# Attention with a deeper lag between scores and transposed probabilities: (1, 5, 7) to (1, 6, 8), eight probability tiles, a fourth conversion buffer

## The chip, the cores and the metric

The kernel runs on one core of one Trainium2 chip. The metric is the device time of one execution in microseconds. Three executions of the kernel before took 909.98, 910.92 and 910.42 us (median 910.42). Times and the trace are of one core; its engines are TensorE (PE, with its weight loads PEld), VectorE (DVE), ScalarE (ACT), GpSimd (POOL), and SyncE (SP), which issues most transfers.

## What is computed

Three layers follow one another: block-causal attention, a feed-forward layer with a squared ReLU, and a layer of eight experts of which each token takes one.

```python
# q, k, v: (4, 8, 576, 64); x: 2304 tokens x 512
scores = scale * np.matmul(q, k.transpose(0, 1, 3, 2))
scores = np.where(block_i >= block_j, scores, -1e9)       # blocks of 64 positions
attn = np.exp(scores - np.max(scores, axis=-1, keepdims=True))
attn = attn / (np.sum(attn, axis=-1, keepdims=True) + 1e-09)
x = (attn @ v)  # heads side by side -> (2304, 512)
g = s * np.maximum(x @ w_in, 0.0) ** 2 + b                # w_in 512 x 2048, float64 on arrival
x = g @ w_out
# then: gate, argmax over 8 experts, out[mask] = gate * (relu(x[mask] @ w1[e]) @ w2[e])
```

## The kernel before

**Attention.** Two heads of one batch make a unit `u`; there are 16 units. A unit has nine query blocks `i` of 64 rows (two heads side by side fill 128 rows), so there are 144 pairs `(u, i)`, and block `i` has `64 * (i + 1)` keys. The loop at L230 takes one step `t` for each pair, and a few steps more to empty the pipeline. In a step it calls, in this order:

- `p_transpose` for the pair `LT` steps back (L231 to L235): PE transposes the probabilities by chunks of 128 keys (L185) into one of three PSUM banks, and ACT copies them to SBUF (L191). Blocks 0 to 3 go in twos.
- `scores` for the pair of this step (L238): POOL zeroes the ragged end of the probability tile (L135), PE multiplies (L143 or L146, three passes) into one of four PSUM banks, DVE takes the maximum (L148, for the last block two halves and L151), ACT takes the exponential with its sum (L153). The last block takes two banks.
- in steps 4 to 6 of a unit the transposes of the next unit's q and k (L93, L123), and the loads of later units on SP (L75, L76, for v with a POOL memset at L67).
- `normalise` for the pair `LN` steps back (L255): DVE forms the reciprocal of the sum (L162 or L164, then L165), POOL multiplies the tile by it (L166).
- `pv` for blocks 3 and 8 of the unit `LP` steps back (L258 to L261): PE multiplies the transposed probabilities by v (L208), ACT copies the result (L210), and after block 8 SP stores the unit (L213).

The lags are in one line, with the number of probability tiles below it:

```python
LAGS = (1, 5, 7)     # LN, LT, LP (L279)
NPBUF = 6            # buffers of the pool a_p, tag "p" (L280)
```

**The feed-forward layer beside it.** The kernel's main loop (L310) runs one step of attention and then, at steps 8, 12, ..., 80 (`CONV`), one step of `convert` (L361): a weight chunk arrives as float64 (L327 on SP), three integer instructions on DVE make float32 of it (L336 to L338, into a tile of the pool `cv`), ACT rounds it to a high part (L371), and POOL subtracts to get the low part (L342). The three stages of one chunk stand in three successive conversion steps. From step 50 on, one "piece" is put behind an attention step every 2.8 steps: a load of 256 tokens (L318, L321, L322), a hidden group (`hidden`, 24 matmuls at L385, then L395 to L398), or a projection (L460). There are 40 pieces; the last ones follow the attention loop. Then `after` (L488) runs the rest of the layer, starting with tokens of the last batch, which need every unit stored.

**Order.** The framework places instructions on the engines' queues when the program is built, earlier program order first among what it reckons ready; on the chip each queue is in order. SBUF tiles of one pool and tag share that pool's buffers, and a new tile waits until its buffer's last reader is done.

Of the kernel before, what the change touches and what calls it, by code (L numbers as in the profile page):

```python
# [20 lines left out]
def attention(nc, tc, ctx, ps, ident, q, k, v, xT_d):  # L21
# [15 lines left out]
    kt = pool("a_kt", 2)  # L37
    pp = pool("a_p", NPBUF)
    small = pool("a_small", 8)
# [175 lines left out]

    LN, LT, LP = LAGS
    QK, V = (("q", q), ("k", k)), (("v", v),)
# [58 lines left out]
            setattr(self, n, ctx.enter_context(p))  # L276


LAGS = (1, 5, 7)  # L279
NPBUF = 6  # L280
PTBUF = 1
BANKS_0 = (4, 3, 1)
P_COPY = lambda nc, i: nc.scalar.copy
# [2 lines left out]
class SquaredRelu:  # L286
# [175 lines left out]

    def beside(self, ctx, blocks):

        self.pools(ctx, "a", 1, 2, max(NA), "raw cv xr x r g")
        rows = ctx.enter_context(self.tc.tile_pool(name="ma_rows", bufs=1))
        return self._beside(blocks, rows)

# [108 lines left out]
NA = (2, 4, 4, 4, 4, 4)  # L577
# [802 lines left out]
```

## Time and profile before

| | us |
|---|---|
| median of three executions | 910.42 |
| the profiled execution | 910.26 |
| its span, first to last instruction | 908.6 |
| time around the span | 1.7 |
| PE busy in the span | 878.3 (97%) |
| DVE busy | 640.3 (70%) |
| ACT busy | 569.9 (63%) |
| POOL busy | 219.9 (24%) |

Attention runs from the start to about 328 us. The granted TensorE clock is at full speed throughout (0.998 of it in the mean). Busy time in the table is a union over the instructions of an engine; an engine's idle time stands before the instruction that it waited with, and the engine and line whose end released it follow the arrow.

### The profile page before, as it was taken

The numbers are of one execution on the slowest core, as the hardware profiler recorded it, in microseconds if no ns is written. First come the engines' busy times: TensorE is split into PE (matmuls) and PEld (weight loads), VectorE is DVE, ScalarE is ACT, GpSimd is POOL, SyncE is SP. The second block draws the span as 40 slices with busy tenths as digits, with TensorE's granted clock in tenths as the row PEclk, the third lists the DMA queues.
The fourth block names the chain that finished last, engine by engine and source line by source line (L and its number), as shares of the span: only waits on it lengthen the run. The fifth ranks groups of instructions, "written<-read, shape, count | busy, mean of one in ns | idle before, by whom it ended". The sixth has DMA issues, their size and how long they took to land. (4 is left out here: it accounts for less than half of the span.)

```text
span 908.6 us, 17050 instructions
## 1 busy us (share of the span) xinstructions
PE 878.3 (97%) x5765; PEld 725.4 (80%) x5765; DVE 640.3 (70%) x1490; ACT 569.9 (63%) x1165; POOL 219.9 (24%) x335
## 2 busy tenths in 40 slices
PE   6889999999999999999999999999999999999996
PEld 5666777888878789999999999998467776776775
DVE  5889986464645446878967777767688887776782
ACT  6888786575757544333566655542288777776773
POOL 4677675142333200000000000002025322222110
PEclk9999999999999999999999999999999999999999
DMA  5766543322221133445212212115346796637500
GB/s 138 181 178 184 143 116 78 100 53 76 77 72 29 53 109 104 157 140 175 59 47 69 71 61 60 47 47 190 119 139 232 239 386 236 224 129 257 188 24 28
DMA packets 109481, 113.84 MB, mean 125 GB/s; under 512 B 62679, under 2 KB 80617, under 8 KB 109387
## 3 DMA queue, kind: packets, MB, share of 16 engines
q1 hardware_dynamic: 105579, 100.74, 35.3%
q0 software_dynamic: 3808, 11.94, 3.7%
q8 instruction: 48, 0.79, 0.4%
q14 instruction: 46, 0.38, 0.1%
HBM read 143.58 MB, written 19.80 MB: 180 GB/s over the span
## 5 line engine op out<-in xcount | busy, mean ns | idle before, releaser
L385 PE MATMUL ph<-xh,wih 128*128 128x256 f32 x576 | 165.9, 288 | 0.0
L385 PE MATMUL ph<-xh,wil 128*128 128x256 f32 x576 | 162.2, 282 | 0.0
L385 PE MATMUL ph<-xl,wih 128*128 128x256 f32 x576 | 162.0, 281 | 0.0
L166 POOL TENSOR_TENSOR p<-p,rc 128x64 f32<-128x64 f32 (+2 forms) x144 | 111.5, 783 | 119.8 <-DVE rc L165 56.7
L385 PEld LDWEIGHTS ph<-xh,wih 128*128 128x128 f32 x576 | 109.0, 189 | 5.3 <-issue 3.1
L385 PEld LDWEIGHTS ph<-xl,wih 128*128 128x128 f32 x576 | 109.2, 189 | 1.1
L385 PEld LDWEIGHTS ph<-xh,wil 128*128 128x128 f32 x576 | 109.2, 190 | 0.4 <-issue 0.4
L148 DVE TENSOR_REDUCE nm<-sc 128x1 f32<-128x288 f32 (+8 forms) x160 | 70.4, 450 | 54.3 <-PE sc L146 46.1
L153 ACT ACTIVATE p<-sc,nm 128x288 f32<-128x288 f32 (+8 forms) x160 | 80.6, 507 | 18.5 <-DVE nm L148 8.0
L1009 DVE TENSOR_TENSOR w1l<-raw,w1h 128x1024 fp32r<-128x1024 f32 x60 | 71.7, 1223 | 22.8 <-ACT w1h L1008 17.8
L1009 DVE TENSOR_TENSOR w2l<-raw,w2h 128x1024 fp32r<-128x1024 f32 x64 | 75.2, 1220 | 9.6 <-ACT w2h L1008 9.5
L1017 POOL DMA_INDIRECT xr<-x_d,gidx_e x2 | 2.3, 1130 | 310.4 <-PE ph L385 310.1
L185 PE MATMUL tp<-ident,p 128*128 128x128 f32 x400 | 65.3, 278 | 6.8 <-POOL p L166 4.9
L395 ACT ACTIVATE r<-ph 128x512 f32<-128x512 f32 x44 | 26.3, 597 | 72.0 <-PE ph L385 71.9
L1008 ACT CAST w2h<-raw 128x1024 fp32r<-128x1024 f32 x64 | 66.1, 1050 | 6.1 <-PE py L1106 5.9
L1008 ACT CAST w1h<-raw 128x1024 fp32r<-128x1024 f32 x60 | 61.6, 1051 | 9.4 <-PE ph L1091 8.7
L191 ACT COPY pt<-tp 128x512 f32<-128x512 f32 (+3 forms) x128 | 61.7, 499 | 8.8 <-PE tp L185 8.4
L185 PEld LDWEIGHTS tp<-ident,p 128*128 128x128 f32 x400 | 46.1, 142 | 18.7 <-POOL p L166 9.2
L396 DVE SCALAR_TENSOR_TENSOR r<-r,sc 128x512 f32<-128x512 f32 x44 | 34.7, 789 | 36.3 <-ACT r L395 36.0
L208 PE MATMUL o<-pt,raw_v 128*64 128x320 f32 (+4 forms) x448 | 55.9, 366 | 1.1 <-ACT pt L191 1.1
L1106 PE MATMUL py<-w2h,hh 128*128 128x512 f32 x128 | 51.6, 403 | 0.0
L1117 POOL DMA_INDIRECT out_dram<-y,sidx x15 | 19.8, 1323 | 130.5 <-ACT y L1073 128.7
(306 smaller groups left out, 2300.6 us busy)
## 6 DMA issues: line engine op xcount, KB each, us to landing
raw<-in_moe_w_dram SPq DMA_DIRECT2D x172, 512.0 KB
xr<-xT_d SPq DMA_DIRECT2D x19, 512.0 KB
wr<-in_moe_w_in_dram SPq DMA_DIRECT2D x16, 512.0 KB
wr<-in_moe_w_out_dram SPq DMA_DIRECT2D x16, 512.0 KB
row<-part_d SPq DMA_DIRECT2D x20, 256.0 KB
x_d<-row SPq DMA_DIRECT2D x18, 256.5 KB
xT_d<-x SPq DMA_DIRECT2D x16, 288.0 KB
raw_q<-in_q_dram SPq DMA_DIRECT2D x32, 128.0 KB
```

Source lines behind the costliest of these rows:

```text
L148: ps.last["max"] = nc.vector.tensor_reduce(nm[:, e:e + 1], sc[:, 0:w], AX.X, ALU.max, negate=True)
L153: ps.last["exp"] = nc.scalar.activation(pr[:, k0:k0 + w], scs[e][:, 0:w], AF.Exp, bias=nm[:, 0:1], accum_out=sm[:, e:e + 1])
L166: ps.last["scale"] = nc.gpsimd.tensor_mul(pr[:, 0:n], pr[:, 0:n], rc.to_broadcast([P, n]))
L185: nc.tensor.transpose(t[:, e * P:(e + 1) * P], st[u][i][0][:, c * P:(c + 1) * P], ident)
L191: P_COPY(nc, i0)(o, src)
L208: nc.tensor.matmul(o[r, first * D:n], vt[:, c, hh], p[:, first:, c, r], start=(c == 0), stop=(c == cs[-1]))
L385: nc.tensor.matmul(ph[:, e], self.wi[p][w][:, c, e * P:(e + 1) * P], x[a][:, c], start=(n == 0), stop=(n == 3 * KC - 1))
L395: nc.scalar.activation(r, ph.rearrange("p e (t n) -> p (e t) n", n=P), AF.Relu)
L396: nc.vector.scalar_tensor_tensor(r, r, self.sc[:, 0:1], r, ALU.mult, ALU.mult)
L1008: self.nc.scalar.copy(ws[0][c], r)
L1009: self.nc.vector.tensor_sub(ws[1][c], r, ws[0][c].bitcast(F32))
L1106: nc.tensor.matmul(py, hT[a][:, c], self.w2s[w][c // 2][:, c % 2 * D:c % 2 * D + D], start=(t == 0), stop=(t == 3 * KF - 1))
```

## The change

The lags become 1, 6 and 8: transposes are called six steps behind their scores and the product with v eight steps behind, two steps apart as before. The pool of probability tiles has eight buffers instead of six (each 2.5 KB in a partition). The pool `cv` of the conversion that runs beside attention has four buffers instead of three (each 2 KB). The conversion of the later stage keeps its two. The loop has one step more.

```diff
-LAGS = (1, 5, 7)
-NPBUF = 6
+LAGS = (1, 6, 8)
+NPBUF = 8
 PTBUF = 1
 BANKS_0 = (4, 3, 1)
...
     def beside(self, ctx, blocks):
 
-        self.pools(ctx, "a", 1, 2, max(NA), "raw cv xr x r g")
+        self.pools(ctx, "a", 1, 2, max(NA), "raw cv xr x r g", 4)
```

## Rows read from the trace of the kernel before

**Rows 1.** Busy us by stretch: stretch, length, PE, PEld, DVE, ACT, POOL, clock, DMA.
```profile
30.00:90.00 60.00, 51.45 (x372) 39.28 (x372) 53.14 (x167) 52.37 (x166) 42.97 (x72) 1.00 0.64 177
90.00:150.00 60.00, 57.31 (x412) 46.69 (x412) 50.79 (x159) 48.31 (x150) 41.82 (x70) 1.00 0.49 132
150.00:330.00 180.00, 179.76 (x1247) 150.61 (x1246) 90.00 (x273) 110.70 (x311) 52.32 (x101) 1.00 0.21 61
```

**Rows 2.** Groups of PE, 30 to 90 us: count, busy, mean ns, idle before, releasers.
```profile
L185 PE MATMUL tp<-ident,p 128*128 128x128 f32 x104 | 17.4, 280 | 5.5 <-POOL p L166 4.4 <-ACT pt L191 0.7 <-POOL wil L342 0.3
L208 PE MATMUL o<-pt,raw_v 128*64 128x320 f32 (+4 forms) x112 | 13.3, 366 | 1.1 <-ACT pt L191 1.1
L146 PE MATMUL sc<-kh,qh 128*128 128x288 f32 (+5 forms) x35 | 13.2, 376 | 1.2 <-ACT p L153 1.2
```

**Rows 3.** The same view of PE, 10 to 30 us.
```profile
L185 PE MATMUL tp<-ident,p 128*128 128x128 f32 x27 | 4.7, 283 | 0.5 <-POOL p L166 0.5
```

**Rows 4.** The same view of ACT and DVE, 30 to 90 us.
```profile
L153 ACT ACTIVATE p<-sc,nm 128x288 f32<-128x288 f32 (+8 forms) x40 | 20.1, 506 | 3.3 <-DVE nm L148 1.1 <-DVE rc L164 1.1 <-DVE rc L165 0.9
L191 ACT COPY pt<-tp 128x512 f32<-128x512 f32 (+3 forms) x32 | 15.2, 500 | 3.4 <-PE tp L185 3.3
...
L148 DVE TENSOR_REDUCE nm<-sc 128x1 f32<-128x288 f32 (+8 forms) x41 | 18.0, 452 | 4.0 <-PE sc L146 3.4 <-PE sc L143 0.4
L336 DVE TENSOR_SCALAR f<-wr 128x512 int32<-128x512 int32 x9 | 6.8, 759 | 1.1 <-POOL wol L342 1.1
```

**Rows 5.** Timeline: start, us, engine, line, [idle before]: first score, first hidden matmul.
```profile
7.71 0.95 PE L143 MATMUL sc<-kf,qf 128*128 128x64 f32 x3
...
89.67 0.36 PE L385 MATMUL ph<-xh,wih 128*128 128x256 f32 x1
```

**Rows 6.** Timeline round two of the waits for POOL, with the exponentials that free banks.
```profile
37.02 0.19 ACT L153 ACTIVATION_READ_ACCUMULATOR p<-sc,nm 128x1 f32 x1
37.79 0.33 PE L146 MATMUL sc<-kh,ql 128*128 128x384 f32 x1
38.96 0.77 PE L185 MATMUL tp<-ident,p 128*128 128x128 f32 x5 [0.83 <-POOL p L166]
...
51.75 0.33 PE L146 MATMUL sc<-kh,ql 128*128 128x384 f32 x1
52.73 0.19 ACT L153 ACTIVATION_READ_ACCUMULATOR p<-sc,nm 128x1 f32 x1
53.35 0.77 PE L185 MATMUL tp<-ident,p 128*128 128x128 f32 x5 [1.27 <-POOL p L166]
```

**Rows 7.** Timeline round a wait for an exponential.
```profile
33.90 0.68 DVE L338 SCALAR_TENSOR_TENSOR f<-wr,f 128x512 int32<-128x512 int32 x1
34.50 0.15 DVE L151 TENSOR_TENSOR nm<-nm 128x1 f32<-128x1 f32 x1
35.58 0.39 PE L146 MATMUL sc<-kh,qh 128*128 128x256 f32 x1 [1.17 <-ACT p L153]
```

**Rows 8.** One line's durations (ns min/median/max), 30 to 90 and 328 to 430 us.
```profile
L336 DVE TENSOR_SCALAR f<-wr x9: 401/696/1269, 32.0 to 81.2; 128x512 int32<-128x512 int32 x9
L336 DVE TENSOR_SCALAR f<-wr x16: 418/421/426, 328.4 to 425.5; 128x512 int32<-128x512 int32 x16
```

**Rows 9.** Timeline: a load of v, and the product of that unit.
```profile
59.72 0.20 POOL L67 MEMSET raw_v<- 64x128 f32 x1
...
76.83 0.87 PE L208 MATMUL o<-pt,raw_v 128*64 128x256 f32 x8
```

**Rows 10.** Timeline at the end of attention.
```profile
325.47 2.27 PE L208 MATMUL o<-pt,raw_v 128*64 128x320 f32 x20
...
330.67 0.37 SPq L318 DMA_DIRECT2D xr<-xT_d  x1
...
338.44 0.38 PE L385 MATMUL ph<-xh,wih 128*128 128x256 f32 x1
...
346.13 0.39 PE L460 MATMUL pxa<-woh,gl 128*128 128x512 f32 x1
```

## The prediction

> **What bounds the kernel now.** I read the busy times by stretch first [rows 1]. From 150 to 330 us PE is idle for 180 - 179.76 = 0.24 us: there PE's own work sets the pace, and the change takes none away and adds none. From 90 to 150 us PE is idle for 2.7 us, from 30 to 90 for 8.55 us. So whatever the change can win lies ahead of 150 us, and nearly all of it ahead of 90. A microsecond of PE idle time removed there is a microsecond of the kernel, since PE is full behind it.
>
> In the 60 us from 30 to 90 no engine is the plain bound: DVE is busy for 53.1 us, ACT for 52.4, PE for 51.45 [rows 1]. The next view is who makes PE wait there. Of the 8.55 us, 5.5 stand before the transposes of the probabilities, 4.4 of them for POOL's normalised tile and 0.3 for POOL's conversion; 1.1 stand before the product with v, 1.2 before scores that wait for an exponential to free a bank [rows 2]. In the 20 us before, 0.5 more are waits for POOL [rows 3]. The same standstill is seen from the other side on ACT and DVE: the copy of the transposes waits 3.3 us for PE, the maximum 3.8 us for scores that are queued behind the waiting transpose [rows 4]. So the loop is coupled: PE, held up by POOL, starves DVE and ACT, which in turn make POOL late.
>
> **The change part by part.** *The transposes one step later.* The first score starts at 7.71 us and the first hidden matmul, a piece of step 53, at 89.67 [rows 5], so a step takes (89.67 - 7.71)/53 = 1.55 us. The longest wait for POOL on PE's queue is 1.27 us [rows 6]; one step more of lag is longer than any of them, so this wait goes altogether: 4.4 + 0.3 + 0.5 = 5.2 us.
>
> What is late next? In place of the transposes PE would go on with the next scores, and those need a bank, of which there are four. Both stalls shown stand behind the scores of block 5; the next score, of block 6, takes the bank of block 2, which its exponential frees. In the first stall PE stands from 38.12 us (37.79 + 0.33) and that exponential is done at 37.21: the bank is free, and all of the 0.83 us is won. In the second PE stands from 52.08 and the exponential is done at 52.92, so only 53.35 - 52.92 = 0.43 of 1.27 us is won [rows 6]. Together 1.26 of 2.10, or 60%. I apply that to all: 0.6 x 5.2 = 3.1 us. A cap comes from the other engines: if ACT and DVE keep the rest of their idle time, the stage shrinks by the smaller of what they wait for PE, 3.3 and 3.8 us [rows 4]; 3.1 is just under it. The bounds are 0 (each wait replaced by one for a bank) and 5.2 us.
>
> *The product with v one step later, and the drain.* PE's work of one step, transposes and products, moves out of the stretch where PE has gaps into the one where it has none. By their busy times it is at most (17.4 + 13.3) us over 60/1.55 = 39 steps, 0.8 us [rows 2]. Against that, ACT's copies of one step move out of the same stretch, and ACT is short of time there. The bounds are 0 and +0.8; I take +0.6.
>
> At the end of attention, the last product ends at 327.7 us; its store, the load of the next tokens (issued at 330.67) and their rounding follow, and the first matmul on them comes at 338.44. PE fills this with pieces, which last until 346.5 [rows 10]. From 338.44 on there are still about 7 us of them. One step later in the program, the product changes places with at most one hidden piece, 24 matmuls, or 2.7 us at the 0.11 us apiece of that product (20 in 2.27 us). About 4 us of cover stay, so this costs nothing; with the cover gone it would be the rest of the 10.7 us chain. On SP the store is issued one step later, and what is queued behind it (a weight chunk and the token load) moves with it.
>
> *The v buffers.* A load of v may start when the product two units before is done, which now comes one step later; POOL's memset waits there with the normalising multiplies of the next blocks behind it, and on SP the loads behind v's wait too. The v loaded at 59.72 us is used at 76.83 [rows 9]; with 17 us between them a step of 1.55 us is hidden. The multiplies behind the memset have the extra step of lag themselves. 0, at worst +0.5 us.
>
> *Eight tiles instead of six.* A tile is now free again two or one steps before its next use, instead of one or none. It removes waits of POOL's memset and costs only memory. 0.
>
> *The fourth conversion buffer.* DVE waited once, 1.1 us, for POOL to be done with a conversion tile [rows 4]. That wait goes. PE had scores and transposes queued at the time, so between 0 and 1.1 us is won; I take 0.2, since DVE then only gets to its next wait sooner.
>
> The profiled execution took 910.26 us (span 908.6 and 1.7 around it), 0.16 us below the median. The sum: 910.26 - 3.1 + 0.6 - 0.2 = **907.6 us**.
>
> One row speaks for a smaller gain. The first conversion instruction takes 0.42 us in the stretch in which POOL is idle, and 0.76 in the mean, up to 1.27, from 30 to 90 us [rows 4, 8], where POOL is busy for 43 of 60 us [rows 1]: DVE loses 9 x 0.34 = 3 us on this line to POOL's presence. The Trainium skill has a rule for it (SBUF — State Buffer, "The single rule" and the notes on reading its diagram): VectorE and GpSimd share one pair of ports, held for a whole instruction, and the other engine blocks. By it a shorter stage packs the same POOL work more densely (5% more in 57 us), and of DVE's 3 us some 0.2 us more would be lost: 907.8 us. The trace's spread of 0.40 to 1.27 us for one shape agrees with it.
>
> **The rivals.** *The wait only changes its name (chance 0.27).* The planner's order moves, but PE then waits for exponentials, as in the second stall [rows 6], where two thirds of the time would be lost again; DVE and ACT, at 89 and 87%, are the loop's real pace. For it: both have 3 to 4 us of idle time that PE does not cause. Against it: the first stall, where the bank was free. Counting every stall as the second one (0.43 of 1.27) gives 1.8 us, less 0.6: 909.1 us; with none won, 910.9. Here belongs also that the planner already places transposes where it reckons them ready, so that one step more in the program moves little in the queues.
>
> *DVE's conversions hold up the exponentials (0.24, slower).* The three conversion instructions stand ahead of the combined maximum of a unit's last block; it ends at 34.65, the exponential waits for it, and PE stands for 1.17 us [rows 7]. With a conversion tile always free, the planner can place such a run earlier on DVE's queue, and with the lag changed it falls on other blocks. It happens in one unit of the four between 30 and 90 us. The price is 1.2 us for each unit hit; nine units are converted beside, up to 144 us. It decides from the third unit on, which eats the 2.7 us won. With five units hit: 907.6 + 4 x 1.2 = 912.4 us.
>
> *The loop comes loose (0.13).* All 5.2 us and the 1.1 us on DVE go, nothing takes their place: 904.0 us. Against it: DVE would be busy for 53.1 of 54 us, with ACT beside it at 97%.
>
> **How the numbers follow.** The forecast has 0.36, with a range of its own of 906.3 to 908.9. With 0.13 for the loose loop, 0.27 for the renamed wait (908.9 to 911) and 0.24 for the conversions (911 to 914), the range that holds 8 in 10 is 904.8 to 912.8: it leaves out some of the loose loop and the worse half of the conversions' case. A difference of 0.2%, 1.8 us, is about what a measurement of this kernel can tell from no change. Below 908.6 lie the loose loop and nearly all of the forecast: 0.47. Above 912.2 lie two thirds of the conversions' case and a little of the others, for orders that the trace of before cannot show: 0.19. Between them 0.34.
>
> **What would show it.** In the changed profile, between 30 and 90 us, the transposes' wait for POOL should be gone (4.4 to under 1 us), the scores' wait for the exponential should rise from 1.2 to about 3, ACT's wait for the transposes fall below 1.5 of its 3.3 us, and the first hidden matmul should come at about 87 instead of 89.7. DVE's wait for POOL's conversion should be gone. PE's idle time from 150 to 330 us should stay under 0.5 us, and the chain behind the last product should still be covered. Wrong would be: PE idle in 30 to 90 us as before with another name (first rival), or several waits for the exponential of a last block, one a unit (second). A change of PE's idle time behind 330 us would be something that I have not counted.

## The result: 916.2 us, 0.7% slower, all of it lost beside attention

The changed kernel took 916.17 us (median; 915.82 to 916.89), the kernel before 910.67 (six runs, 909.95 to 911.23): a ratio of 1.0069, 95% interval 1.0058 to 1.0080. I had forecast 907.6 us, with 904.8 to 912.8 as the range. The profiled execution took 916.09 us with a span of 914.4, 5.8 us more than before. (One execution of the changed kernel and one of `after_q_copies_late`, both at a throttled clock, are left out of ranges and ratios; the medians count them, which moves them by less than 0.3 us.)

First, where the time lies. Timelines of PE, the changed kernel: start in us, duration, engine, line.

```profile
89.91 0.28 PE L385 MATMUL ph<-xh,wih 128*128 128x256 f32 x1
...
331.06 2.27 PE L208 MATMUL o<-pt,raw_v 128*64 128x320 f32 x20
...
352.15 0.39 PE L460 MATMUL pxa<-woh,gl 128*128 128x512 f32 x1
```

The first hidden piece comes when it came before [rows 5]; the last product is 5.6 us later, the last projection beside attention 6.0 us later [rows 10]. The span is 5.8 us longer, so nothing is lost behind that: of the loss, 0.2 us stand ahead of the first hidden piece and some 5.4 between it and the last product. Busy time by stretch, in the columns of [rows 1]:

```profile
30.00:90.00 60.00, 53.78 (x372) 40.38 (x369) 55.21 (x168) 52.41 (x168) 44.29 (x68) 1.00 0.63 169
90.00:150.00 60.00, 57.41 (x400) 45.60 (x398) 48.12 (x149) 45.83 (x140) 37.05 (x68) 1.00 0.49 128
150.00:330.00 180.00, 178.31 (x1222) 149.48 (x1221) 90.19 (x277) 110.41 (x317) 52.38 (x104) 1.00 0.23 64
```

By idle time the change looks like a gain: from 30 to 90 us PE is idle for 6.2 us instead of 8.55 [rows 1]. Yet the first piece is no earlier, and from 150 to 330 us PE gets through fewer matmuls (1222 instead of 1247) although it is nearly always busy. From 90 to 330 us, where most of the loss arises, PE is idle for 4.3 us instead of 2.9. So most of the loss sits inside "busy": the page's first part gives PE 884.8 us instead of 878.3, for as many instructions.

```profile
PE 884.8 (97%) x5765; PEld 728.5 (80%) x5765; DVE 642.4 (70%) x1490; ACT 569.6 (62%) x1165; POOL 217.5 (24%) x335
```

The groups of PE, 30 to 90 us, as in [rows 2]:

```profile
L208 PE MATMUL o<-pt,raw_v 128*64 128x320 f32 (+4 forms) x122 | 17.6, 362 | 0.5 <-ACT pt L191 0.5
L185 PE MATMUL tp<-ident,p 128*128 128x128 f32 x98 | 16.8, 279 | 3.0 <-ACT pt L191 2.2 <-POOL p L166 0.6
L146 PE MATMUL sc<-kh,qh 128*128 128x288 f32 (+5 forms) x33 | 12.8, 388 | 0.5 <-ACT p L153 0.5
L93 PE MATMUL tw<-ident,raw_k 128*128 128x128 f32 x16 | 2.6, 286 | 1.4 <-ACT pt L191 1.4
```

The transposes' wait for POOL fell from 4.4 to 0.6 us, as forecast. In its place stand waits for ACT's copy of earlier transposes (L191), which frees a bank: 2.2 us before the probabilities' transposes, 1.4 before k's. And the product (L208) takes 17.6 us for 122 matmuls instead of 13.3 for 112. Over the whole of attention (0 to 350 us) its 448 matmuls are busy for 4.5 us more, first the changed kernel, then the kernel before:

```profile
L208 PE MATMUL o<-pt,raw_v 128*64 128x320 f32 (+4 forms) x448 | 60.4, 366 | 0.5 <-ACT pt L191 0.5
```

```profile
L208 PE MATMUL o<-pt,raw_v 128*64 128x320 f32 (+4 forms) x448 | 55.9, 366 | 1.1 <-ACT pt L191 1.1
```

The views of PE's waits from 0 to 350 us (total us, times, longest), first the changed kernel, then the kernel before:

```profile
PE tp L185 <- ACT pt L191: 4.6, 12, 0.9
PE tw L93 <- ACT pt L191: 2.5, 4, 1.0
PE tp L185 <- POOL p L166: 0.6, 1, 0.6
```

```profile
PE tp L185 <- POOL p L166: 4.9, 7, 1.3
PE tp L185 <- ACT pt L191: 0.7, 3, 0.3
```

ACT and DVE, 30 to 90 us, answering to [rows 4]:

```profile
L153 ACT ACTIVATE p<-sc,nm 128x288 f32<-128x288 f32 (+8 forms) x41 | 20.9, 516 | 2.9 <-DVE rc L164 1.5 <-DVE nm L148 1.1 <-DVE rc L165 0.2
L191 ACT COPY pt<-tp 128x512 f32<-128x512 f32 (+3 forms) x31 | 15.4, 504 | 2.8 <-PE tp L185 2.7
...
L336 DVE TENSOR_SCALAR f<-wr 128x512 int32<-128x512 int32 x10 | 7.5, 751 | 0.3 <-DMA wr<-in_moe_w_out_dram 0.3
```

### The profile page after: what moved, and what is told of

Read it like the earlier page. It is cut to its first block, busy times and chain, and to the rows that moved or that the text cites. A ratio compares the mean times of both kernels' runs of the same rounds, so it can differ in the third digit from the quotient of the medians.

```text
span 914.4 us, 17032 instructions
## 1 busy us (share of the span) xinstructions
PE 884.8 (97%) x5765; PEld 728.5 (80%) x5765; DVE 642.4 (70%) x1490; ACT 569.6 (62%) x1165; POOL 217.5 (24%) x335
## 5 line engine op out<-in xcount | busy, mean ns | idle before, releaser
L148 DVE TENSOR_REDUCE nm<-sc 128x1 f32<-128x288 f32 (+8 forms) x160 | 70.7, 450 | 53.6 <-PE sc L146 47.0
L185 PE MATMUL tp<-ident,p 128*128 128x128 f32 x400 | 66.8, 278 | 6.9 <-ACT pt L191 4.6
L191 ACT COPY pt<-tp 128x512 f32<-128x512 f32 (+3 forms) x128 | 62.4, 499 | 14.0 <-PE tp L185 13.3
L185 PEld LDWEIGHTS tp<-ident,p 128*128 128x128 f32 x400 | 46.1, 142 | 21.7 <-issue 8.0
L208 PE MATMUL o<-pt,raw_v 128*64 128x320 f32 (+4 forms) x448 | 60.4, 366 | 0.5 <-ACT pt L191 0.5
```

The source lines that it names most:

```text
L148: ps.last["max"] = nc.vector.tensor_reduce(nm[:, e:e + 1], sc[:, 0:w], AX.X, ALU.max, negate=True)
L185: nc.tensor.transpose(t[:, e * P:(e + 1) * P], st[u][i][0][:, c * P:(c + 1) * P], ident)
L191: P_COPY(nc, i0)(o, src)
L208: nc.tensor.matmul(o[r, first * D:n], vt[:, c, hh], p[:, first:, c, r], start=(c == 0), stop=(c == cs[-1]))
```

## The experiments

Their order: which edit, then which coincidence inside it, then why that costs. The expectations name PE's waits "by starts". That is a sum worked out from the traces: for successive matmuls, the distance of their starts beyond the usual distance for that shape, put down to what released the later one or its weight load, up to the last projection beside attention. It also sees waits that lie inside modelled busy time, and it moves by 1 to 2 us with what is taken as the usual distance. Times are medians, with the ratio to the kernel before as run beside it and its 95% interval.

### Which of the three edits

**Four conversion buffers alone** (`cv4_alone`: the kernel before with `"raw cv xr x r g", 4`).

> The kernel before with four conversion buffers. Theories A and B: 910 to 911 us, at most 0.5 us less, for DVE's one wait of 1.1 us for POOL. Theory C: 913 to 917 us.

Measured: 909.67 us, 1.0001 (0.9991 to 1.0010). Nothing.

**Eight tiles alone** (`np8_alone`: the kernel before with `NPBUF = 8`).

> The kernel before with eight probability tiles instead of six and nothing else. Bank theory: 909 to 911 us, the waits as before, since no tile's bank changes. Rival (the tiles themselves, by their place in memory or by letting POOL's memset and ACT's exponentials run ahead): a change of over 2 us either way.

Measured: 910.74 us, 1.0011 (1.0001 to 1.0021); by starts PE's waits stay where they were (7.8 us for POOL, 3.9 for the copies). At most 0.2%.

**The lag with three conversion buffers** (`lag_cv3`: the changed kernel without the 4).

> The changed kernel with three conversion buffers as before: lag six and eight tiles alone. Theories A and B: as the changed kernel, 914 to 917 us. Theory C: the loss goes, 909 to 911 us.

Measured: 916.31 us, 1.0075 (1.0058 to 1.0092), waits for the copies 11.5 us as in the changed kernel. With the eight tiles alone at 0.1%, the loss belongs to the lag.

### The lag, or what it meets

At lag 5 block 8's transposes are called in step 4 of the following unit, and in the same step, behind them, those of a later unit's q. With lag 6 they are called in step 5: q now goes ahead of them.

**q, k and tails moved along** (`later_qk`).

```diff
-                    if i == 4:
+                    if i == 5:
                         q_transpose(u + 1)
-                    if i == 5:
+                    if i == 6:
                         k_transpose(u + 1)
-                if i == 6:
+                if i == 7:
                     tails(u + 1)
```

> The changed kernel, with the transposes of the next unit's q, k and tails called in steps 5, 6 and 7 of a unit instead of 4, 5 and 6. In the changed kernel PE stood 10.9 us (22 times) before transposing matmuls until ACT had copied an earlier transposed tile out of its PSUM bank (3.2 us, 11 times, in the kernel before). Theory A (phase): with a lag of six the two transposed tiles of a unit's last block fall into the step in which k is transposed, and three, later two, banks don't hold them; one step later restores the phase of the kernel before, so that this wait falls to about 3 to 5 us, the waits for POOL stay short (under 2 us) and the time is 907 to 911 us. Theory B (lag as such: copies of transposes stand one step later on ACT's queue, whatever the phase): about as the changed kernel, 915 to 917 us, with 9 us or more of that wait. Theory C (the fourth conversion buffer lets DVE's conversions run ahead): about 915 to 917 us too, with the wait for the transposes' copies anywhere.

Measured: 910.75 us, 1.0009 (0.9999 to 1.0019). The loss is gone with lag, tiles and buffers all as changed. PE's transposes, 30 to 90 us:

```profile
L185 PE MATMUL tp<-ident,p 128*128 128x128 f32 x100 | 16.3, 278 | 4.6 <-ACT pt L191 1.7 <-POOL p L166 1.6 <-DVE ql L86 1.2
```

The wait for POOL is down here too (1.6 instead of 4.4), yet nothing is won: 4.6 us stand before the transposes under three names, against 5.5 under mostly one before [rows 2].

**The same conflict at the old lag** (`earlier_qk`: the kernel before with q, k and tails at steps 3, 4 and 5).

> The kernel before (lags 1, 5, 7, six tiles, three conversion buffers), with the transposes of the next unit's q, k and tails called in steps 3, 4 and 5 instead of 4, 5 and 6: the phase of the changed kernel without its lag. Theory A (phase): transposing matmuls wait for ACT's copies as in the changed kernel, 8 to 11 us instead of 3.2, and the waits for POOL stay about 7 us, so 914 to 918 us. Theory B (lag) and theory C (conversion buffer): no such wait beyond 5 us and 909 to 912 us.

Measured: 917.14 us, 1.0080 (1.0063 to 1.0097). The loss comes without any change of the lag. Here the waits for the copies were only 6.9 us by starts; so their sum is not a measure of the loss.

### A failed guess: tiles in a step, or banks in number

I first took it for a matter of how many transposed tiles fall into one step.

**k one step later** (`after_k_apart`: the changed kernel with k at step 6 and the tails at 7) and **q and k one step earlier** (`after_qk_first`: the changed kernel with q at 3, k at 4).

> The changed kernel with q transposed in step 4 as before, k in step 6 (which has no transposes of probabilities at a lag of six) and the tails in step 7. Transposed tiles asked for in steps 4 to 7: 2, 2, 1, 2, where the changed kernel has 2, 3, 1, 1 and the kernel before 3, 1, 2, 1 in its steps 4 to 7. Bank theory: the wait for the transposes' copies is at most that of the kernel with all three later (4.4 us), and 907 to 911 us. Rival (it matters only that q is not with block 7): as the changed kernel, 914 to 917 us.

> The changed kernel with q in step 3, k in step 4 and the tails in step 6: ahead of the last block's two tiles, which have step 5 for themselves. Tiles asked for in steps 3 to 7: 2, 2, 2, 1, 1. Bank theory: the wait for copies is under 6 us and the time 907 to 912 us. Rival (k and q have to come after the last block's tiles, as in the kernel before, since their banks are held until DVE has made the low parts): 914 us or more.

Measured: 916.99 us (1.0086, 1.0069 to 1.0103) and 915.28 us (1.0062, 1.0046 to 1.0079). Neither spreading helps.

**One bank more for transposes, one less for scores** (`after_t_banks`).

```diff
-BANKS_0 = (4, 3, 1)
+BANKS_0 = (3, 4, 1)
...
-BANKS_A = (3, 2, 1)
+BANKS_A = (2, 3, 1)
```

> The changed kernel with one PSUM bank taken from the scores and given to the transposes: (3, 4, 1) instead of (4, 3, 1) up to step 36, (2, 3, 1) instead of (3, 2, 1) from there. Bank theory: the wait of transposing matmuls for ACT's copies falls from 10.9 us to under 5, at the price of waits of scores for exponentials (1.7 + 1.0 us in the changed kernel), which may cost as much or more in the first 150 us: 908 to 916 us. Queue theory (ACT is overloaded in the steps where the copies of the last block meet those of q and k, and PE is late whatever it waits for): the wait moves to scores altogether, and the time stays at 915 to 918 us.

Measured: 921.51 us, 1.0131 (1.0114 to 1.0148), beyond what either theory allowed. The probabilities' wait for copies is gone from the head of its list of waits (0 to 350 us), but the scores now wait for exponentials, and POOL's waits are back:

```profile
PE tp L185 <- POOL p L166: 3.6, 7, 1.1
PE tw L93 <- ACT pt L191: 3.1, 6, 1.4
PE sc L146 <- ACT p L153: 2.8, 5, 1.1
PE sc L143 <- ACT p L153: 2.7, 5, 1.2
```

So this run says what the scores lose with a bank less, and not that a further bank for transposes would be worth nothing.

### The order of q and the last block

All slow kernels so far have q's transposes ahead of block 8's, all others behind. The next four test just that.

**One swap within a step**, at lag 6 (`later_q_ahead`) and at lag 5 (`before_q_ahead`): `q_transpose` is called in the same step as `later_qk` and the kernel before call it, but ahead of `p_transpose`. The diff is that of `before_q_ahead`; in `later_q_ahead` the step is 5.

```diff
+        u, i = at(t)
+        if i == 4 and u + 1 < NU:
+            with tc.issue_after(ps.last["exp"].ins) if u == 0 else nullcontext():
+                q_transpose(u + 1)
         u, i = at(t - LT)
         if i in (1, 3):
             p_transpose(u, [i - 1, i])
...
-                    if i == 4:
-                        q_transpose(u + 1)
```

> later_qk (q's, k's transposes and the tails called at steps 5, 6 and 7, 910.75 us) with one swap: within step 5 q's transposes are called ahead of the transposes of block 8, not behind them. Lags, buffers and steps are the same. Theory 'order': q's tile holds a transposes' bank until ACT has made four copies of it, so the two tiles of block 8 behind it find no bank, and their copies stand behind q's on ACT's queue: 915 to 917 us, PE's waits for the copies at L191 from 5.8 to 10 us or more. Rival 'step': only the step counts in which q falls, the order within it is evened out: 910 to 911.5 us, waits about 6.

> The kernel before with the same swap alone: q's transposes are still called at step 4, but ahead of those of block 8 in that step; k at 5, tails at 6, lags and buffers as before. Theory 'order': 914 to 917 us, PE's waits for the copies at L191 from 4.1 to 9 us or more, without any change of the lag. Rival 'step': 909.5 to 910.5 us, waits 4 to 5.

Measured: `later_q_ahead` 915.60 us, 1.0064 (1.0047 to 1.0081), `before_q_ahead` 914.13 us, 1.0044 (1.0030 to 1.0059). The swap alone costs 5 and 4 us; it is the order that counts, not the step and not the lag.

**q one step behind the last block**, at lag 6 (`after_qk_678`: steps 6, 7, 8) and lag 5 (`before_qk_567`: steps 5, 6, 7).

> The changed kernel with q, k and tails at steps 6, 7 and 8: q falls into the step behind block 8's transposes, one step farther than in later_qk. Theory 'order': q stands behind block 8, so 909.5 to 911.5 us and waits for the copies at L191 of 4 to 7 us. Rival 'step': q has to share block 8's step, any other is slow: 914 us or more; with the tails in the unit's last step the next unit's scores may also wait for k's end (L117, L118), which would show as waits of the scores for ACT or DVE, 1 us a unit.

> The kernel before with q, k and tails at steps 5, 6 and 7: lag 5, q in the step behind block 8's transposes. Theory 'order': not slower than before, 908.5 to 910.5 us, waits for the copies at L191 of 3 to 5 us. Rival 'step': 914 us or more, waits of 8 us or more.

Measured: 908.57 us, 0.9985 (0.9976 to 0.9995), and 908.30 us, 0.9978 (0.9968 to 0.9989). Both are faster than the kernel before, by some 0.2%, and the 0.3 us between them are within the spread of their runs. Both times lie a little below what theory 'order' expected, with more waits for the copies than it expected (7.7 and 7.0 us by starts); why one step more behind block 8 gains is open.

Worked out from the traces of these fourteen kernels: in how many of 14 units the first transpose of q (L93) starts ahead of the last transpose of block 8 (L185) on PE; in how many uninterrupted sequences PE runs the 32 products with v; the waits for the copies by starts; the time.

```
kernel           lag  q ahead  sequences  copies us   time us
before_qk_567     5    0/14       42         7.0       908.30
after_qk_678      6    0/14       43         7.7       908.57
cv4_alone         5    0/14       42         4.0       909.67
before            5    0/14       42         4.1       910.67
np8_alone         5    0/14       42         3.9       910.74
later_qk          6    0/14       42         5.8       910.75
before_q_ahead    5   14/14       55        11.0       914.13
after_qk_first    6   14/14       44        10.4       915.28
later_q_ahead     6   14/14       51        14.1       915.60
changed kernel    6   14/14       48        11.5       916.17
lag_cv3           6   14/14       48        11.5       916.31
after_k_apart     6   14/14       50        13.0       916.99
earlier_qk        5   14/14       53         6.9       917.14
after_t_banks     6   14/14       42         6.8       921.51
```

(The times are of several comparisons; the kernel before beside them took 909.5 to 910.7 us.) The order splits these fourteen without exception; no other column does, and the lag doesn't. (It does not split the kernels of the next section, whose edits cost time of their own.) The timelines show what follows from the order. First `before_q_ahead`, PE, ACT and DVE:

```profile
35.69 0.60 PE L93 MATMUL tw<-ident,raw_q 128*128 128x128 f32 x4
...
37.44 0.66 PE L185 MATMUL tp<-ident,p 128*128 128x128 f32 x4 [0.72 <-POOL p L166]
...
37.60 0.29 ACT L102 ACTIVATE qf<-tw 64x128 f32<-64x128 f32 x1
37.76 0.51 ACT L105 ACTIVATE qh<-tw 64x384 fp32r<-64x384 f32 x1
...
38.46 0.48 ACT L105 ACTIVATE qh<-tw 64x384 fp32r<-64x384 f32 x1
...
38.67 0.27 PE L185 MATMUL tp<-ident,p 128*128 128x128 f32 x1
...
38.96 0.76 ACT L191 COPY pt<-tp 128x512 f32<-128x512 f32 x2
...
39.92 1.11 DVE L86 SCALAR_TENSOR_TENSOR ql<-tw,qh 64x384 fp32r<-64x384 f32 x2
...
40.61 0.75 PE L208 MATMUL o<-pt,raw_v 128*64 128x320 f32 x2
...
41.55 2.27 PE L208 MATMUL o<-pt,raw_v 128*64 128x320 f32 x18
```

q's tile is written from 35.69 us and its last reader (L86) ends at 41.03: it holds one of three banks for 5.3 us. (In the mean of units 1 to 15 that is 4.6 us here and 4.1 in the kernel before, so what differs most is what stands behind it.) Block 8's five transposes are torn apart (four at 37.44, the fifth at 38.67), and the copies of their two tiles stand behind q's four on ACT, until 39.72. The product after them is cut: two of its matmuls at 40.61, and 18 from 41.55 on, with another transpose between. In the kernel before, block 8's five transposes go together [rows 6], and its copies precede q's. In the same unit its product is cut too, but as 16 and 4; the next one is whole:

```profile
39.56 0.60 PE L93 MATMUL tw<-ident,raw_q 128*128 128x128 f32 x4
39.65 0.75 ACT L191 COPY pt<-tp 128x512 f32<-128x512 f32 x2 [0.70 <-PE tp L185]
...
40.29 0.28 ACT L102 ACTIVATE qf<-tw 64x128 f32<-64x128 f32 x1
...
41.35 2.16 PE L208 MATMUL o<-pt,raw_v 128*64 128x320 f32 x16
...
43.70 0.34 PE L208 MATMUL o<-pt,raw_v 128*64 128x64 f32 x4
...
55.98 2.28 PE L208 MATMUL o<-pt,raw_v 128*64 128x320 f32 x20
```

So it is not that one kernel cuts its products and the other doesn't (`before_q_ahead` has its next product whole as well): there are more cuts, and they fall elsewhere. Nor is a cut a wait on the chip, as the order of the queues is that of the build: the swap changed PE's queue itself.

A cut has a price of its own, which no view calls idle. From the product's first matmul to the matmul behind its last it is 2.20 us for the whole product, 2.62 for the one cut as 16 and 4, and 3.14 for the one cut as 2 and 18, the transpose between included. From 30 to 90 us the product takes, in `before_q_ahead`,

```profile
L208 PE MATMUL o<-pt,raw_v 128*64 128x320 f32 (+4 forms) x112 | 16.3, 367 | 0.5 <-ACT pt L191 0.5
```

16.3 us for the same 112 matmuls that took 13.3 [rows 2].

Worked out from the traces, from the first matmul of each sequence to the matmul behind it, summed: 59.5 us in `before_q_ahead` against 55.2 in the kernel before, and 58.3 in `later_q_ahead` against 53.6 in `later_qk`. These 4.3 and 4.7 us are about what the two swaps cost. But `after_qk_first` loses 5.8 us with 55.3, so longer products are not the loss of every kernel with this order.

### Why the order costs: not settled

Besides the cuts on PE's queue, two resources could carry it: the bank that q's tile holds, or ACT's queue, where q's copies stand ahead of block 8's.

**q's tile in another bank**: it takes the one bank of the product. In the changed kernel (`after_q_own_bank`), the kernel before (`before_q_own_bank`) and `later_qk` (`later_q_own_bank`).

```diff
-    def transpose4(src):
-        t = ps.t.tile([P, 512], F32, name="tw", tag="t")
+    def transpose4(src, pool=None, tag="t"):
+        t = (pool or ps.t).tile([P, 512], F32, name="tw", tag=tag)
...
-        q_high(u, transpose4(st[u]["raw"][0]), slice(0, 8))
+        q_high(u, transpose4(st[u]["raw"][0], ps.o, "o"), slice(0, 8))
```

> The changed kernel with one edit: q's transposed tile takes the one PSUM bank of the product with v (free from step 3 to 6 of a unit, between two products) instead of one of the transposes' banks; the order of calls, the lags and ACT's copies are the same. Theory 'bank': the loss comes from q's tile holding a bank (4 to 6 us) that the last block's tiles need, so it goes: 908 to 911.5 us, PE's waits for the copies at L191 from 11.5 to 6 us or less. Rival 'ACT's queue': the last block's copies stand behind q's four on ACT, whichever bank q has: 914 us or more, waits of 9 us or more.

> The kernel before with the same edit. Theory 'bank': q also costs something there, as it follows the last block's tiles into the same banks: 907 to 909.5 us, waits for the copies at L191 from 4.1 to 3 us or less; the product of the next step may wait for the bank by up to 1 us a unit in the first units. Rival 'ACT's queue': as before, 909 to 910.5 us.

> later_qk (changed kernel with q, k and tails at steps 5, 6 and 7) with q's tile in the product's bank. The product of block 8 comes at step 7, two steps behind q, so the bank is still free in time. Theory 'bank': 907.5 to 910.5 us, a little below later_qk's 910.75. Rival 'ACT's queue': 910 to 911.5 us. If it is near before_q_own_bank, one step more of lag is worth nothing when the banks are no obstacle either; if 1.5 us or more below, the lag has its gain only there.

Measured: 914.53 us (1.0059, 1.0040 to 1.0077), 914.79 us (1.0051, 1.0032 to 1.0070) and 915.74 us (1.0064, 1.0046 to 1.0081). In the changed kernel most of the added cuts go (43 sequences instead of 48), the waits for the copies fall from 11.5 to 9.1 us, and 1.6 us come back by the medians, 0.9 by the ratios, whose intervals overlap. But the edit costs some 5 us in the other two, where q stood behind block 8 (and now slips ahead of it in 4 and 3 of 14 units). In `before_q_own_bank` (waits of PE, 0 to 350 us) the product waits for q's last reader, and scores for exponentials:

```profile
PE sc L146 <- ACT p L153: 4.2, 6, 0.9
...
PE o L208 <- DVE ql L86: 2.9, 6, 0.9
```

So my claim that the product's bank is free in time was wrong, and the runs don't tell bank from queue: 914.53 us is what the rival 'ACT's queue' expected, while the distance to the kernel before with the same edit is gone (0.3 us below it), as 'bank' would have it, but because that kernel lost 5 us.

**q's copies alone behind block 8's** (`after_q_copies_late`: `after_q_own_bank`, with the four copies and the low part of q called at step 5, behind `p_transpose`).

> after_q_own_bank (914.5 us) with one edit: q's transposes stay at step 4 and ahead on PE, in the product's bank, but ACT's four copies of them are called at step 5, behind the copies of block 8's transposes. Theory 'ACT's queue': the time comes back, 909 to 912 us, PE's waits for the copies at L191 from 9.1 to 6 us or less. Rival 'PE's order': q's transposes ahead of block 8's cost by their place on PE or by the bank held, so 914 us or more, whatever stands on ACT.

Measured: 921.82 us, 1.0125 (1.0106 to 1.0143), 7 us worse than `after_q_own_bank`. On ACT block 8's copies now precede all four of q's in 9 of 14 units and three of the four in 4 more, and it doesn't help. That speaks against "ACT's queue"; but q now holds the product's bank until the later copies are made. (Its waits are not compared here.)

**Block 8's copies on DVE**, in the changed kernel (`after_block8_dve`) and the kernel before (`before_block8_dve`).

```diff
-P_COPY = lambda nc, i: nc.scalar.copy
+P_COPY = lambda nc, i: nc.vector.tensor_copy if i == 8 else nc.scalar.copy
```

> The changed kernel with the two copies of block 8's transposes on DVE instead of ACT, so that they can't stand behind q's copies on ACT; order and banks as in the changed kernel. Theory 'ACT's queue': most of the loss is gone against the next run, that is 1 to 2 us between the two kernels where 6.3 us lay before. Rival 'bank': q's tile still holds its bank, 4 us or more between the two. DVE has some 7 us idle time in 60, and the copies put 1 to 1.3 us a unit on it, so both kernels may be slower by some us.

> The kernel before with the two copies of block 8's transposes on DVE: the control of the run before it. Both theories: 909 to 915 us, by what DVE's queue bears; only the distance to the changed kernel with the same edit tells the theories apart (1 to 2 us for 'ACT's queue', 4 or more for 'bank').

Measured: 916.39 us (1.0075, 1.0058 to 1.0093) and 915.28 us (1.0053, 1.0036 to 1.0070). The distance is 1.1 us, as "ACT's queue" expected, but because the control lost 4.8 us, not because the changed kernel gained. Its products are cut as well (49 sequences), and in the changed kernel POOL's waits are back (0 to 350 us):

```profile
PE tp L185 <- POOL p L166: 3.5, 5, 1.7
```

Two kernels at 915 to 916 us for different reasons prove nothing about the first. That the order costs 4 to 5 us is shown by the two swaps; how that divides among the bank, ACT's queue and the cut products is open.

## Why the prediction was wrong

- **The wait for POOL** goes: right, 4.4 to 0.6 us, at the forecast place.
- **"What is late next"** is the step that failed, twice. I asked only which bank the next *score* would find, and took 60% as won. What came next was a *transpose* without a bank: PE's idle time for scores' banks fell (L146 from 1.2 to 0.5 us, where a rise to about 3 was forecast) and that for transposes' banks rose from 0.7 to 2.2. And the gain of 3.1 us isn't there even where the order is right: `later_qk` has the whole change and no conflict, for which the sum had -2.7 us, and is 0.8 us above the kernel before beside it, interval -0.1 to +1.7 (the +0.6 for the drain was not measured by itself); `after_qk_678` and `before_qk_567` differ by 0.3 us. The lag by itself renames its wait, which was my first rival, though not to the wait for exponentials that it named (ACT's copies, POOL and DVE's low part of q share it, 4.6 us); its 909.1 to 910.9 us fit `later_qk`'s 910.75.
- **The loss** was in none of my cases. I moved the transposes by a step and went through the queues of SP and POOL that they pass, but not PE's and ACT's: that the move takes block 8's tiles from ahead of q's to behind them stands in the loop's order of calls, which I had described. The swap has a measured price of 4 us (lag 5) or 5 us (lag 6); with the lag's own 0 to 1 that is the 5.5 us.
- **DVE's conversions** as the slower case (0.24): not the cause. `lag_cv3` has three buffers and is as slow. DVE's wait for POOL's conversion went as forecast (L336, 1.1 us before [rows 4]), and was worth nothing (`cv4_alone`): the -0.2 is not there.
- **Other marks.** ACT's wait for the transposes fell from 3.3 to 2.7 us, not below 1.5; the first piece came at 89.9 us, not 87; PE's idle time from 150 to 330 us was 1.7 us, not under 0.5. These three spoke against the forecast at once. The end of attention cost nothing, as reckoned, and eight tiles next to nothing.
- **Idle time as the purse.** I reckoned nearly all in waits of PE, most of them ahead of 90 us (up to 144 in the conversions' case). Most of the loss came behind 90 us and was no idle time: cut products and short waits lengthen PE's busy time, also where it is never idle.
- The 0.2 us that I put beside the sum by the Trainium skill (SBUF — State Buffer, "Who interferes with whom", "The single rule") can't be seen: the stage did not get shorter, and DVE's first conversion took 751 ns in the mean against 759 [rows 4].

## What to carry to other kernels

A lag in a software pipeline is also a phase: moving one stage by a step changes which other work, sharing its banks and queues, it stands ahead of. Before changing a lag, write out the order of calls in a step before and after, and look for pairs on one pool or one engine that swap; move them along, or try the swap alone. And count matmuls got through in a stretch, not PE's idle time: here idle time fell while the stage became longer.

## What the runs showed of the hardware

A product of 64-column matmuls (128*64 in the rows) can be dear to interrupt, and it matters where. In the whole product at 55.98 us the 20 matmuls stand in ten pairs of one width, starts within 10 ns, by the order of calls one of each head. The two ahead of the cut in `before_q_ahead` (40.61 us) started 0.32 us apart, and behind the cut, from 42.68 us on, a matmul of 320 columns stands beside one of 192: the two were of one head, which from there on is a chunk ahead of the other, and the other's last ones start alone, to 43.60 us. The cut into 16 and 4 leaves all pairs together. In the sums above, 13 more sequences came with 4.3 us more, so about a third of a microsecond a cut.

In one place the clock fell as well. In `earlier_qk` a product followed transposes for which PE had waited 1.54 and 0.61 us; busy times by stretch (columns as in [rows 1]; the granted clock is the last but two), and the timeline:

```profile
80.00:86.00 6.00, 4.46 (x28) 3.24 (x26) 5.75 (x17) 5.57 (x18) 5.04 (x8) 1.00 0.57 151
...
88.00:91.00 3.00, 3.00 (x16) 1.75 (x13) 2.80 (x5) 0.75 (x4) 2.31 (x2) 0.51 0.51 144
```

```profile
85.14 0.33 PE L185 MATMUL tp<-ident,p 128*128 128x128 f32 x1 [1.54 <-ACT pt L191]
...
86.77 0.66 PE L93 MATMUL tw<-ident,raw_k 128*128 128x128 f32 x4 [0.61 <-DVE ql L86]
...
87.46 3.96 PE L208 MATMUL o<-pt,raw_v 128*64 128x320 f32 x18
```

The granted clock fell to 0.51, the 1.2 GHz level, and 18 matmuls took 3.96 us instead of the 2.27 above. The changed kernel's clock reads 1.00 in all three stretches from 30 to 330 us, so this is no part of its loss.
